# An attention and mixture-of-experts kernel: sums of weight quarters formed earlier and in buffers of their own, a ring of six, and tokens gathered a layer ahead

## The chip, the cores and the metric

The kernel runs as one program on one core of a Trainium2 chip. The metric is device time in microseconds (us) from launch to end. The profiled execution is one run of its own, and its rows give the times at which instructions ran on TensorE (PE, with PEld for the loading of weights), VectorE (DVE), ScalarE (ACT), GpSimd (POOL) and on the issue queue of SyncE (SP).

## The reference

Inputs are float32. Attention on pooled keys and values makes 4608 tokens of 512; each token goes to one of 8 experts (576 tokens each), whose two layers are applied; then a third, common layer with a squared relu and a last product follow.

```python
def _attn_ref(q, k, v):                       # B=8, H=8, S=576, D=64, pool=8
    k_p = k.reshape(B, H, Sp, pool, D).mean(axis=3)
    v_p = v.reshape(B, H, Sp, pool, D).mean(axis=3)
    scores = scale * np.matmul(q, k_p.transpose(0, 1, 3, 2))
    ...
    return np.matmul(attn, v_p)
def _moe_ref(x, w_gate, w1, w2):              # N=4608, D=512, E=8, F=1024
    cap = N // E
    logits = x @ w_gate
    order = np.argsort(-logits.flatten())
    ...                                       # greedy: best pairs first, cap tokens an expert
    for e in range(E):
        mask = assigned == e
        out[mask] = np.maximum(x[mask] @ w1[e], 0.0) @ w2[e]
def _moe2_ref(x, w_in, w_out):                # 512 -> 2048 -> 512
    r = np.maximum(x @ w_in, 0.0)
    return (r * r) @ w_out
```

## The kernel before

**Stages.** `attention` writes the tokens to memory and the gate's logits to `L`; then `mlp(n)` runs for the experts n = 0 to 7, one after the other. Every number that enters a product is split into two float16 parts, and each product takes three passes (`PASSES`). Layer 1 (weights `e1`, tokens `xy`) and layer 2 (weights `e2`, hidden values `hs`) are matrix products through `layer`, line 1250. Layer 3 multiplies by the common `w_in`; its result `g` is multiplied by `w_out` (tile `wo`) in `last_layer`, line 1438, and the rows are scattered to the output.

**Layer 3.** Expert 0 computes it as a plain product with the parts of `w_in` in the tile `wi`. Experts 1 to 7 use a Strassen-Winograd scheme with seven products instead of eight for each of 4 column groups (`ORDER`, `FACTORS`, function `product`, line 1382); their results are put together on ACT (`copy`, `relu`) and DVE (`join` line 1403, `square` line 1408). The scheme needs four sums of quarters of `w_in`. `mix_first` forms them once: 16 pieces, each read from memory (`begin`, line 721), added up on POOL (lines 744 to 747), split by ACT (732) and POOL (733) and stored to `mixed_weights` (737). Layer 3 then reads its weights from there through a ring of `WS` buffers (`fetch_sum`, line 1274). The pieces, the ring and the gathered tokens all lie in the space of `wi`, which expert 0 needs until its layer 3 ends; so `mix_first` waits for `("l3", 0)`, and expert 1 waits for `"mixed"` ahead of its layer 3.

**Background work.** While products run, generators give out other work: `routes` (which tokens go to expert n; small DVE steps with a matmul between them, lines 808 to 1050), `feed` and `fetch(n)` (the expert's weights: loads line 1069, squares on ACT 1079, a column sum on PE 234, splitting on ACT 1092 and DVE 1093, first w1, and then w2 through the same buffer `hs`), and `tokens` and `gather(n)` (gathering by POOL line 1156, splitting 1189 and 1190 into `gfm`, transposing by DMA 1191). The buffer `hs` is also the one that layer 1 writes its result to.

**What sets the order.** All engines work in the order in which the code gives out instructions. The class `Background` keeps an estimate of how far PE, ACT, DVE and POOL have come (`pe`, `a`, `v`, `p`). `tick` advances a task while its engines are no more than `depth` us ahead of PE by this estimate; a task names its engines ("av" for `feed` and `tokens`, "rv" for `routes`, "ap" for `mix_first`). In layer 3 `depth` is `NEAR` = 1.2, most ticks hold back tasks that use ACT (`hold="a"`), and `slot(0.9)` and `slot(3.0)` open all tasks once a group each. `wait_next(n)` stands ahead of each expert's layer 1: it gives out what is still missing of the expert's w1, w2 and tokens.

## Time and profile before

| | us |
|---|---|
| median of 3 runs | 1467.92 (1464.05 to 1469.99) |
| profiled execution, its own time | 1471.88 |
| its span, first to last instruction | 1469.4 |
| PE busy | 1310.9 (89%) |
| DVE busy | 906.6 (62%) |
| ACT busy | 636.3 (43%) |
| POOL busy | 444.9 (30%) |

The attention stage takes about the first 190 us; expert 0 runs from 236 us, expert 1 from 407 us, expert 2 from 594 us, and expert 7 starts at 1319 us. A row of the timeline gives start, length, engine, line, what is written and read, and in square brackets how long the engine had stood still just ahead of it and what ended that.

### The profile page before, as it was taken

Reading aid. Unit: us, or ns where it says so; the run is one execution under the profiler, and the core shown is the slowest. Engines: PE = TensorE matmul, PEld = TensorE weight load, DVE = VectorE, ACT = ScalarE, POOL = GpSimd, SP = SyncE. Lnnn points to the kernel's source line nnn. Section 1 sums busy time; section 2 is a strip of 40 time slices with the busy share of each in tenths; the row PEclk is TensorE's granted clock in tenths of the full one; section 3 lists DMA queues with packets and bytes.
Section 4 is the critical chain, followed back from the end, with each engine's and each line's share of the span. In section 5 each row is a group of like instructions: output and inputs, shape, how many; then the busy total and the mean of one; then the engine's idle time right before and its main releaser. Section 6 shows DMA issues by size and latency. Waiting matters only on the chain.

```text
span 1469.4 us, 25459 instructions
## 1 busy us (share of the span) xinstructions
PE 1310.9 (89%) x9925; PEld 928.7 (63%) x9925; DVE 906.6 (62%) x2203; ACT 636.3 (43%) x1241; POOL 444.9 (30%) x449
## 2 busy tenths in 40 slices
PE   6999927989794798998899789999999999999997
PEld 5989826765373653775367535774677477647753
DVE  6797997888477684678667966473246314622520
ACT  4776756544433452144433442264336414632520
POOL 4552041235556341024302431143015102510430
PEclk8997957999897899999999999999999999999999
DMA  8877457003644634023531451064314602470400
GB/s 339 331 307 271 172 186 234 1 1 112 169 101 118 187 116 119 8 72 130 138 84 58 145 156 60 1 201 136 87 53 153 197 15 83 147 191 4 129 30 21
DMA packets 138872, 186.09 MB, mean 127 GB/s; under 512 B 74624, under 2 KB 88960, under 8 KB 134016
## 3 DMA queue, kind: packets, MB, share of 16 engines
q1 hardware_dynamic: 127744, 156.15, 33.8%
q0 software_dynamic: 5824, 18.88, 3.9%
q10 hardware_dynamic: 5184, 9.44, 1.7%
q8 instruction: 77, 1.26, 0.4%
q14 instruction: 43, 0.35, 0.1%
HBM read 143.67 MB, written 30.41 MB: 118 GB/s over the span
## 4 chain that ended last, share of the span: by engine, by line
PE 56%; DVE 16%; ACT 5%; issue 4%; DMA 3%; POOL 2%; SPq 0%; POOLq 0%; ACTq 0%; DVEq 0%
PE mm L1250 22%; PE mm L1438 20%; PE mm L1382 13%; DMA xy<-gfm 3%; DVE qa L1408 2%; DVE gep L855 1%; DVE gfm L1190 1%; DVE qa L1403 1%; ACT gfm L1189 1%; DVE e L1093 1%; POOL wi L733 1%; DVE hs L1285 1%; DVE rf L851 1%; DVE wi L1408 1%; DVE rfb L859 0%
## 5 line engine op out<-in xcount | busy, mean ns | idle before, releaser
L1438 PE MATMUL mm<-wo,g 128*128 128x512 f16 x1728 | 393.3, 387 | 0.0
L1250 PEld LDWEIGHTS <-e 128*128 128x128 f16 x3024 | 292.4, 98 | 76.0 <-issue 2.5
L1438 PEld LDWEIGHTS <-g 128*128 128x128 f16 x1728 | 169.0, 100 | 217.9 <-issue 24.6
L1382 PEld LDWEIGHTS <-wi 128*128 128x128 f16 x2352 | 229.5, 98 | 89.3 <-issue 29.0
L1250 PE MATMUL mm<-hs,e 128*128 128x288 f16 x1536 | 193.2, 286 | 0.0
L1382 PE MATMUL mm<-wi 128*128 128x288 f16 x1344 | 178.5, 287 | 14.6 <-DVE wi L1403 10.9
L1250 PE MATMUL mm<-xy,e 128*128 128x288 f16 x1488 | 186.4, 286 | 1.1 <-DVE hs L1285 1.1
L1382 PE MATMUL mm<-xy,wi 128*128 128x288 f16 x1008 | 136.3, 289 | 11.5 <-issue 11.1
L1415 POOL TENSOR_TENSOR g<-qa,g 128x576 f16<-128x576 f32 x70 | 99.4, 1426 | 104.8 <-ACT g L1414 100.6
L1285 DVE SCALAR_TENSOR_TENSOR hs<-mm,hs 128x576 f16<-128x576 f32 x64 | 48.1, 754 | 90.7 <-ACT hs L1284 90.7
L1449 POOL DMA_INDIRECT out_dram<-qa,idx x32 | 33.2, 1038 | 228.8 <-ACT qa L1446 228.4
L1284 ACT ACTIVATE hs<-mm 128x576 f16<-128x576 f32 x64 | 41.6, 651 | 130.3 <-PE mm L1250 124.8
L1093 DVE SCALAR_TENSOR_TENSOR e<-hs,e_s,e 128x1024 f16<-128x1024 f32 (+1 forms) x64 | 75.9, 1234 | 27.0 <-ACT e L1092 26.1
L1408 DVE SCALAR_TENSOR_TENSOR qa<-qa 128x576 f32<-128x576 f32 x86 | 76.6, 892 | 13.0 <-ACT qa L1395 8.1
L1399 ACT ACTIVATE qa<-mm,sg_s 128x576 f32<-128x576 f32 x72 | 52.9, 736 | 66.9 <-PE mm L1250 20.2
L1446 ACT ACTIVATE qa<-mm,uo 128x512 f32<-128x512 f32 x32 | 21.9, 685 | 137.1 <-PE mm L1438 122.3
L1079 ACT ACTIVATE e<-hs 128x1024 bf16<-128x1024 f32 x60 | 62.7, 1046 | 38.3 <-DMA hs<-in_w_dram 37.0
L451 ACT ACTIVATE es<-sc,mb 128x72 f32<-128x72 f32 x288 | 64.7, 337 | 31.3 <-DVE mb L449 30.9
L1415 POOL TENSOR_TENSOR g<-wi,g 128x576 f16<-128x576 f32 x42 | 56.8, 1352 | 70.6 <-ACT g L1414 70.6
L1190 DVE SCALAR_TENSOR_TENSOR gfm<-wi,x_s,gfm 128x512 f16<-128x512 f32 (+1 forms) x35 | 26.0, 749 | 81.7 <-ACT gfm L1189 81.5
L1403 DVE SCALAR_TENSOR_TENSOR qa<-mm,sg_s,qa 128x576 f32<-128x576 f32 x56 | 45.5, 813 | 47.2 <-ACT qa L1399 42.3
L1092 ACT ACTIVATE e<-hs,e_s 128x1024 f16<-128x1024 f32 (+1 forms) x64 | 65.8, 1084 | 15.0 <-DVE e_n L223 11.7
(357 smaller groups left out, 1894.2 us busy)
## 6 DMA issues: line engine op xcount, KB each, us to landing
wi<-mixed_weights SPq DMA_DIRECT2D x196, 256.0 KB, 3.1
hs<-in_w_dram SPq DMA_DIRECT2D x60, 512.0 KB, 6.3
tokens_dram<-x ACTq DMA_DIRECT2D x36, 256.0 KB, 4.7
kt<-in_k_dram SPq DMA_DIRECT2D x7, 1152.0 KB, 8.5
vt<-in_v_dram SPq DMA_DIRECT2D x7, 1152.0 KB, 11.3
qt<-in_q_dram SPq DMA_DIRECT2D x7, 1152.0 KB, 5.6
mixed_weights<-wi SPq DMA_DIRECT2D x56, 128.0 KB, 2.0
e<-in_win_dram SPq DMA_DIRECT2D x6, 1024.0 KB, 9.6
```

What stands on the lines that cost most here:

```text
L451: A.activation(es[i][:, x, :], sc[i, x // 4][:, x % 4, :], AF.Exp, scale=1.0 / 64.0, bias=mb[:, x:x + 1])
L1079: A.activation(dst[:, 0, s2, :].bitcast(BF), staged(st, j)[:, s2, :], AF.Square, accum_out=rm[:, c:c + 1])
L1092: A.activation(dst[:, 0], src, AF.Copy, scale=s)
L1093: V.scalar_tensor_tensor(dst[:, 1], src, s, dst[:, 0], op0=OP.mult, op1=OP.subtract)
L1250: T.matmul(p[:, z, 0:HT], lhsT=lh, rhs=mov(b, c)[:, HALVES[z]], start=c == 0 and a + b == 0, stop=c == kk - 1 and a == 1)
L1285: V.scalar_tensor_tensor(halved(h[:, 1, m]), p, 0.0, halved(h[:, 0, m]), op0=OP.max, op1=OP.subtract)
L1382: T.matmul(p[:, z, 0:HT], lhsT=w[:, k, u, z * 128:z * 128 + 128], rhs=yq[:, k, v], start=i in (1, 2, 5) and k == 0 and u + v == 0, stop=k ...
L1399: A.activation(q, p, AF.Copy, scale=sg["r"])
L1403: V.scalar_tensor_tensor(q, p, sg["r"], q, op0=OP.mult, op1=OP.add)
L1408: V.scalar_tensor_tensor(q, q, 0.0, q, op0=OP.max, op1=OP.mult)
L1415: P.tensor_tensor(out=g[:, 1, m:m + 2, gz], in0=q, in1=g[:, 0, m:m + 2, gz], op=OP.subtract)
L1438: T.matmul(o2[c], lhsT=g[:, b, kk, cs], rhs=wo[:, kk // 2, a, kk % 2, :], start=z == 0 and a + b == 0, stop=z == 15 and a == 1)
```

## The change

The buffer `mixb` (three tiles of 128 x 512 float32) is new. `mix_first` puts the pieces there: two buffers for reading, the third for the split sums. It no longer waits for the end of expert 0's layer 3 before it starts on the pieces, only before the first ring loads. Each piece is stored by one DMA whose rows are 256 numbers long instead of two with 128; `product` reads the sums with their indices in the new order. The ring has 6 buffers; the two that fall out and `mixb` hold the gathered tokens from expert 2 on (`xg2`), so `gather(n)` for n > 1 can start ahead of the end of the previous layer 3, and its splitting is spaced by 4 us. `Background` has a second limit, `vdepth`, on DVE alone: 0.9 in layer 3 of experts 1 to 7 and 9.9 elsewhere; `depth` is no longer lowered there.

```diff
-WS = 8
+WS = 6
...
-                   and all(getattr(self, e) <= self.pe + self.depth for e in t[3] if e != "r")):
+                   and all(getattr(self, e) <= self.pe + (min(self.depth, self.vdepth) if e == "v" else self.depth)
+                           for e in t[3] if e != "r")):
...
-    xgs = [wflat.bitcast(F32)[:, o:o + DM] for o in (4096, 4608, 5120, 5632, 6976)]
+    mixb = wt.tile([128, 3, DM], F32)
+    xg1 = [wflat.bitcast(F32)[:, o:o + DM] for o in (4096, 4608, 5120, 5632, 6976)]
+    xg2 = [wflat.bitcast(F32)[:, o:o + DM] for o in (3072, 3584)] + [mixb[:, z] for z in range(3)]
...
-        while ("l3", 0) not in done:
-            yield later()
...
+        parts = mixb[:, 2].bitcast(F16).rearrange("p (s a f) -> p s a f", s=4, a=2)
...
+        for n, (gr, k, z) in enumerate(pieces):
+            flat = mixb[:, n % 2].rearrange("p (q f) -> p q f", q=4)
...
             bg.work(p=2.1)
-            if n:
-                convert(n - 1)
             yield bg.p + 2.0
-        convert(len(pieces) - 1)
+            A.activation(parts[:, :, 0], flat, AF.Copy)
+            P.tensor_tensor(out=parts[:, :, 1], in0=flat, in1=parts[:, :, 0], op=OP.subtract)
+            bg.work(a=0.6, p=1.4)
+            o = k * 512 + z * 256
+            nc.sync.dma_start(out=mix[gr, 3:7, :, o:o + 256].rearrange("s p f -> p s f"),
+                              in_=parts.rearrange("p s a f -> p s (a f)"))
+            yield bg.p
+            if n + 2 < len(pieces):
+                begin(n + 2)
+        while ("l3", 0) not in done:
+            yield later()
...
-        while ("l3", n - 1) not in done:
-            yield later()
+        if n == 1:
+            while ("l3", 0) not in done:
+                yield later()
         for _ in range(NM + 1):
             get()
+        if n > 1:
+            while ("l3", n - 1) not in done:
+                yield later()
+            at = [max(at[c], bg.pe + 4.0 * c) for c in range(NM + 1)]
...
                 if k == 0:
-                    bg.depth = NEAR
                     bg.tick(0.73, hold="a")
...
         b, a, e = mm(), mm(), mm()
+        bg.vdepth = 0.9
...
-            bg.depth = NEAR
             bg.tick(hold="a")
-        bg.depth = DEPTH
+        bg.vdepth = 9.9
```

On POOL, in layer 3 of expert 0, the low parts of `g` (line 1485 before, 1488 after) stood in one row, with the sums behind them (744 to 747, and 733 for the split). Before:

```order
L1485 TENSOR_TENSOR g<-qa,g 128x576 x16
L1156 DMA wi<-tokens_dram,idx_4764 128x512 x4
L1156 DMA wi<-tokens_dram,idl_3141 64x512
L744 TENSOR_TENSOR wi<-wi 128x128
L745 TENSOR_TENSOR wi<-wi 128x128
L746 TENSOR_TENSOR wi<-wi 128x128
L747 TENSOR_TENSOR wi<-wi 128x128
```

After (730 to 733 are the additions, 737 is the split):

```order
L1488 TENSOR_TENSOR g<-qa,g 128x576 x2
L737 TENSOR_TENSOR mixb<-mixb 128x4x128
L1488 TENSOR_TENSOR g<-qa,g 128x576 x2
L730 TENSOR_TENSOR mixb<-mixb 128x128
L731 TENSOR_TENSOR mixb<-mixb 128x128
L732 TENSOR_TENSOR mixb<-mixb 128x128
L733 TENSOR_TENSOR mixb<-mixb 128x128
L1488 TENSOR_TENSOR g<-qa,g 128x576 x2
```

The pieces now lie between the low parts; 8 of the 16 stand ahead of the gathering of expert 1's tokens, and the last one stands in the middle of expert 1's layer 2.

On DVE, in the first column groups of expert 1's layer 3, the splitting of expert 2's w1 (1093) stood between the steps that put the results together (1403 and 1408 before, 1406 and 1411 after). Before:

```order
L1403 SCALAR_TENSOR_TENSOR qa<-mm_2617,sg_s,qa 128x576
L1408 SCALAR_TENSOR_TENSOR qa<-qa 128x576
L1408 SCALAR_TENSOR_TENSOR wi<-wi 128x576
L1408 SCALAR_TENSOR_TENSOR qa<-qa 128x576
L1093 SCALAR_TENSOR_TENSOR e_139<-hs,e_s,e_139 128x1024
L1403 SCALAR_TENSOR_TENSOR wi<-mm_2617,sg_s,wi 128x576
```

After:

```order
L1406 SCALAR_TENSOR_TENSOR qa<-mm_2617,sg_s,qa 128x576
L1411 SCALAR_TENSOR_TENSOR qa<-qa 128x576
L1411 SCALAR_TENSOR_TENSOR wi<-wi 128x576
L1411 SCALAR_TENSOR_TENSOR qa<-qa 128x576
L971 TENSOR_TENSOR roq<-rqi,row 128x576
L1406 SCALAR_TENSOR_TENSOR wi<-mm_2617,sg_s,wi 128x576
```

No splitting of weights stands there any more; a step of the routing does.

On SP, from expert 3's layer 3 to the next expert, the loads of expert 4's w1 (1069 before, 1063 after) stood among the ring loads (1274 before, 1273 after). Before:

```order
L1274 DMA wi<-mixed_weights 128x1024 x7
L1115 TENSOR_LOAD ei_8131
L1115 ISA x2
L1069 ISA
L1069 DMA hs<-in_w_dram 128x1024
...
L1274 DMA wi<-mixed_weights 128x1024 x13
```

After:

```order
L1273 DMA wi<-mixed_weights 128x1024 x28
L1190 DMA_TRANSPOSE xy<-gfm 128x8x128
L1109 TENSOR_LOAD ei_8364
L1109 ISA x2
L1063 ISA
L1063 DMA hs<-in_w_dram 128x1024
...
L1190 DMA_TRANSPOSE xy<-gfm 128x8x128 x3
```

The loads now stand behind the last ring load and the first transpose, so they start when layer 3 is over; this holds at each of the six steps from expert 1 on (at expert 1 the loads stand ahead of all five transposes).

On PE, at the start of expert 3's layer 1, the column sum of w2 (234 before, 236 after) stood some 55 matmuls, of `w_out` and of the routing, ahead of layer 1. Before:

```order
L1438 MATMUL mm_2616<-wo,g 128x512
L234 LDWEIGHTS onesb
L234 MATMUL rp<-rsm_8657,onesb 128x1
L876 LDWEIGHTS gep
L876 MATMUL rp<-oh,gep 128x64
```

After:

```order
L1441 MATMUL mm_2617<-wo,g 128x512
L236 LDWEIGHTS onesb
L236 MATMUL rp<-rsm_8648,onesb 128x1
L1249 LDWEIGHTS e_139
L1249 MATMUL mm_2616<-xy,e_139 128x288
```

It now stands directly ahead of layer 1, as it does for experts 5 and 7; for experts 2, 4 and 6 37 to 48 matmuls still lie between.

## Rows read from the trace of the kernel before

**Rows 1.** Stretches: us, busy of PE, PEld, DVE, ACT, POOL, clock, DMA.
```profile
264.00:350.00 86.00, 76.63 (x651) 59.04 (x649) 74.00 (x186) 36.22 (x56) 30.39 (x22) 0.98 0.02 4
455.00:482.00 27.00, 1.85 (x24) 1.04 (x22) 19.26 (x42) 8.92 (x16) 16.87 (x22) 0.58 0.55 153
```
**Rows 2.** Waits of PE: who waited for whom, us in total, times, longest.
```profile
PE rp L234 <- DVE rsm L230: 11.0, 5, 2.8
PE mm L1382 <- DVE wi L1403: 10.9, 5, 3.5
...
PE mm L1382 <- DVE qa L1403: 3.7, 3, 1.8
```
**Rows 3.** Timeline of PE, end of expert 1's layer 2 to its layer 3.
```profile
453.16 2.37 PE L1250 MATMUL mm<-hs,e 128*128 128x288 f16 x18
...
481.98 1.60 PE L1382 MATMUL mm<-xy,wi 128*128 128x288 f16 x6 [11.09 <-issue]
...
483.66 3.83 PE L1382 MATMUL mm<-xy,wi 128*128 128x288 f16 x18
```
**Rows 4.** Timeline of POOL in the same place, the last splits.
```profile
476.18 2.26 POOL L733 TENSOR_TENSOR wi<-wi 128x512 f16<-128x512 f32 x2 [5.63 <-ACT wi L732]
```
**Rows 5.** Timeline of DVE and of PE in expert 1's layer 3.
```profile
497.95 2.04 DVE L1093 SCALAR_TENSOR_TENSOR e<-hs,e_s,e 128x1024 f16<-128x1024 f32 x1 [1.42 <-ACT e L1092]
...
500.77 2.37 PE L1382 MATMUL mm<-wi 128*128 128x288 f16 x18 [1.40 <-DVE wi L1403]
```
**Rows 6.** Timeline of DVE and of PE in expert 2's layer 3.
```profile
685.16 2.50 DVE L977 TENSOR_TENSOR roq<-rqi,row 128x576 bf16<-128x576 int32 x2
...
688.44 3.04 PE L1382 MATMUL mm<-wi 128*128 128x288 f16 x12 [3.51 <-DVE wi L1403]
```
**Rows 7.** Timeline of PE in the products of `w_out` between experts.
```profile
568.03 0.28 PE L890 MATMUL rp<-rcd,onesh 120*128 120x120 f16 x1 [6.81 <-DVE rcd L885]
...
728.73 0.23 PE L890 MATMUL rp<-rcd,onesh 120*128 120x120 f16 x1 [2.70 <-DVE rcd L885]
...
877.55 0.28 PE L890 MATMUL rp<-rcd,onesh 120*128 120x120 f16 x1 [4.90 <-DVE rcd L885]
877.63 6.51 PE L1438 MATMUL mm<-wo,g 128*128 128x512 f16 x18
...
1026.36 14.59 PE L1438 MATMUL mm<-wo,g 128*128 128x512 f16 x60
```
**Rows 8.** Timeline of SP, DVE and PE between the later experts.
```profile
1138.02 3.98 SPq L1069 DMA_DIRECT2D hs<-in_w_dram  x4
1151.40 10.69 SPq L1191 DMA_TRANSPOSE xy<-gfm  x5
...
1032.38 4.87 DVE L1093 SCALAR_TENSOR_TENSOR e<-hs,e_s,e 128x1024 f16<-128x1024 f32 x4 [5.44 <-ACT e L1092]
...
1161.02 23.47 PE L1438 MATMUL mm<-wo,g 128*128 128x512 f16 x108
...
1319.40 23.68 PE L1250 MATMUL mm<-xy,e 128*128 128x288 f16 x192
```
**Rows 9.** Timeline of SP and of DVE: expert 1's weights, first load to last split.
```profile
347.57 2.13 SPq L1069 DMA_DIRECT2D hs<-in_w_dram  x4
...
402.66 4.87 DVE L1093 SCALAR_TENSOR_TENSOR e<-hs,e_s,e 128x1024 f16<-128x1024 f32 x4
```
**Rows 10.** Single lines: count, ns min/median/max, first and last start.
```profile
L859 DVE SCALAR_TENSOR_TENSOR rfb<-rkm,rfb x42: 145/152/2069, 191.6 to 892.6; 128x1 int32<-128x1 int32 x42
...
L744 POOL TENSOR_TENSOR wi<-wi x16: 452/465/1431, 364.8 to 468.4; 128x128 f32<-128x128 f32 x16
...
L733 POOL TENSOR_TENSOR wi<-wi x16: 1152/1158/1663, 371.7 to 477.3; 128x512 f16<-128x512 f32 x16
```
**Rows 11.** DMA: ring loads (KB, median us to landing); weight loads from 1080 to 1160 us.
```profile
wi<-mixed_weights SPq DMA_DIRECT2D x196, 256.0 KB, 3.1
...
DMA to landing us min/median/max: 4.9/6.6/8.9
```

More of the change, by code (lines that the diff above doesn't have):

```diff
@@ L68, in __init__ @@
         self.depth = DEPTH
+        self.vdepth = 9.9
     def add(self, gen, uses="av"):
@@ L618, in moe_kernel @@
     wflat = wi.rearrange("p c a b f -> p (c a b f)")
-    ring = [wflat[:, z * 1024:z * 1024 + 1024].rearrange("p (k a f) -> p k a f", k=2, a=2) for z in range(WS)]
+    ring = [wflat[:, z * 1024:z * 1024 + 1024] for z in range(WS)]
     yt = wflat[:, 8192:8192 + 16 * HT].rearrange("p (t k a f) -> p t k a f", t=4, k=2, a=2)
@@ L709, in mix_first @@
             yield bg.pe + 1.0
-        while ("l3", 0) not in done:
-            yield later()
         pieces = [(gr, k, z) for gr in range(4) for k in range(2) for z in range(2)]
-        stage = {}
+        parts = mixb[:, 2].bitcast(F16).rearrange("p (s a f) -> p s a f", s=4, a=2)
         def begin(n):
             gr, k, z = pieces[n]
-            o = 512 * (n % 4)
-            stage[n] = wflat.bitcast(F32)[:, o:o + 512].rearrange("p (a b f) -> p a b f", a=2, b=2)
             o = gr * 256 + z * 128
             for a in range(2):
-                nc.sync.dma_start(out=stage[n][:, a], in_=rows4[k, :, a, :, o:o + 128])
+                nc.sync.dma_start(out=mixb[:, n % 2].rearrange("p (a b f) -> p a b f", a=2, b=2)[:, a],
+                                  in_=rows4[k, :, a, :, o:o + 128])
         begin(0)
@@ L725, in mix_first @@
         yield bg.pe + 8.0
-        def convert(n):
-            gr, k, z = pieces[n]
-            o = 4096 + 1024 * (n % 4)
-            parts = wflat[:, o:o + 1024].rearrange("p (a s f) -> p a s f", a=2, s=4)
-            flat = stage.pop(n).rearrange("p a b f -> p (a b) f")
-            A.activation(parts[:, 0], flat, AF.Copy)
-            P.tensor_tensor(out=parts[:, 1], in0=flat, in1=parts[:, 0], op=OP.subtract)
-            bg.work(a=0.6, p=1.4)
-            for a in range(2):
-                o = k * 512 + a * 256 + z * 128
-                nc.sync.dma_start(out=mix[gr, 3:7, :, o:o + 128].rearrange("s p f -> p s f"), in_=parts[:, a])
-        for n in range(len(pieces)):
-            if n + 2 < len(pieces):
-                begin(n + 2)
-            st = stage[n]
-            a11, a21, a12, a22 = (st[:, a, b] for a in range(2) for b in range(2))
+        for n, (gr, k, z) in enumerate(pieces):
+            flat = mixb[:, n % 2].rearrange("p (q f) -> p q f", q=4)
+            a11, a21, a12, a22 = (flat[:, q] for q in range(4))
             P.tensor_tensor(out=a22, in0=a21, in1=a22, op=OP.add)
@@ L1147, in get @@
             if n:
-                t = xgs[c]
+                t = (xg1 if n == 1 else xg2)[c]
             elif c == NM:
-                t = r_p.tile([128, DM], F32, name="xg", bufs=1)
+                t = mixb[:, 2]
             else:
@@ L1273, in fetch_sum @@
         gr, i = ORDER[j]
-        nc.sync.dma_start(out=ring[j % WS].rearrange("p k a f -> p (k a f)"), in_=mix[gr, FACTORS[i][0]])
+        nc.sync.dma_start(out=ring[j % WS], in_=mix[gr, FACTORS[i][0]])
     def mlp(n, arrive=None):
@@ L1377, in product @@
             p = {1: b, 2: a, 3: e, 4: b, 5: e, 6: b, 7: b}[i]
-            w, yq = ring[j % WS], ysum[FACTORS[i][1]]
+            ia, iy = FACTORS[i]
+            w, yq = ring[j % WS], ysum[iy]
+            if ia < 3:
+                w = w.rearrange("p (k a z f) -> p k a z f", k=2, a=2, z=2)
+            else:
+                w = w.rearrange("p (k z a f) -> p k a z f", k=2, a=2, z=2)
             for k in range(2):
@@ L1381, in product @@
                     for u, v in PASSES:
-                        T.matmul(p[:, z, 0:HT], lhsT=w[:, k, u, z * 128:z * 128 + 128], rhs=yq[:, k, v],
+                        T.matmul(p[:, z, 0:HT], lhsT=w[:, k, u, z], rhs=yq[:, k, v],
                                  start=i in (1, 2, 5) and k == 0 and u + v == 0, stop=k == 1 and u == 1,
```

## The prediction

> **What bounds the kernel now.** I read the stretches first, then the waits of PE, then the timeline around each long wait. From expert 0 on, PE is the engine that sets the end: it is busy in nearly every stretch, and the time to be won lies where it stands still. The largest such place is one: from 455 to 482 us PE works 1.85 of 27 us, at a mean granted clock of 0.58 [rows 1]. Layer 2 of expert 1 ends at 453.16 + 2.37 = 455.5 and the first product of its layer 3 starts at 481.98 [rows 3]. What ends last there is POOL's two splits of the last pieces at 476.18 to 478.4 [rows 4], behind which the stores and the first ring loads follow (median 3.1 us to landing, [rows 11]). So 26.4 us pass because the sums of weights are made too late, not because any engine is full.
>
> Smaller standstills repeat. In layer 3 of experts 1 to 3, PE waits eight times, 10.9 + 3.7 = 14.6 us, for `join` on DVE [rows 2]; the rows show what is ahead of it there: a split of w1 of 2.04 us in expert 1 [rows 5], two routing steps of 2.50 us together in expert 2, with a wait of 3.51 [rows 6]. Between the experts PE waits five times, 11.0 us, for the squares of w2 behind the column sum [rows 2], and for routing steps held up on DVE: 6.81, 2.70 and 4.90 us [rows 7]. After some of these the products are slow for a while: 18 take 6.51 us and 60 take 14.59 [rows 7], where 108 take 23.47, 0.217 each, in an undisturbed row [rows 8].
>
> **The change part by part.** All sums go against the profiled execution: 1471.9 us for a span of 1469.4; the median of the three runs, 1467.9, is 4.0 lower, and I carry the same difference over.
>
> *Sums formed earlier.* The code's order puts the last piece 124 of layer 2's matmuls ahead of its end (at 23.68/192 = 0.123 us each, the rate of layer 1, [rows 8], about 15 us), and the first ring loads right behind it. Store and load then need some 6 us of these 15. The whole wait goes: 26.4 us less the 1.85 that PE worked, hence 24.6; and the 24 slow products behind it (1.60 + 3.83 us against 24 x 0.123 = 2.95, [rows 3]) give back 2.5. **Minus 27.1.** What is late next there is nothing that I find: the scale of layer 3 needs the result of layer 2, as before.
>
> *POOL beside expert 0.* A piece costs POOL 4 x 0.465 + 1.158 = 3.0 us [rows 10], and eight pieces, 24 us, now lie in the time from 264 to 350, where POOL has 86 - 30.4 = 55.6 us free [rows 1]. POOL itself is covered. DVE is not: it works 74.0 of these 86 us [rows 1], with routing steps that PE waits for. That DVE instructions can be held far beyond their own time shows in line 859: median 0.152 us, longest 2.069 [rows 10]. Bounds: none of POOL's 24 us reaches DVE and nothing is lost (the pieces also leave the time after 360, where they could hold DVE too), or all of it does, 24. Nearest is the median of line 859, which says that most instructions are not held: I take a quarter. **Plus 6.** The ACT copy waits for POOL's four additions and for the last store out of the one buffer; queued behind it on ACT are the results of layer 3, for which PE has three tiles of room, so I price it at nothing beyond the 6.
>
> The Trainium skill (SBUF — State Buffer, section SBUF: two separate sides) says that VectorE with two inputs in SBUF and a GpSimd instruction that reads SBUF take a shared pair of ports by an exclusive lock, held for the whole instruction, with the loser blocked. This speaks against the change. The row of line 859 agrees with the kind of delay, though not with every instruction being hit; by the rule alone the term would be near its upper bound, which is a rival below.
>
> *The limit on DVE and the weight loads.* In layer 3 the four splits of w1 (4.87/4 = 1.2 us each by [rows 8], one of 2.04 in [rows 5]) no longer stand ahead of `join`, and routing steps get at most 0.9 us of lead; `slot(3.0)` no longer lets DVE run 3 us ahead. Of the 14.6 us I take back 11; bounds 0 (the routing steps that remain, such as those in [rows 6], hold `join` as long as before) and 14.6. **Minus 11.** The routing work that lay in the gap and in layer 3 moves to other places: DVE worked 19.26 us in the gap [rows 1]. Bounds 0 and 19; as the splits of w1 free 4 x 1.2 us of DVE in the same layer 3, and DVE is idle for 38% of the span, it is nearer to none. **Plus 3.**
>
> *Between the experts.* `fetch` wants room on ACT and on DVE, and in layer 3 it no longer finds it; so w1 is loaded only when layer 3 is over. The chain from there: about 3 us to the first transpose, behind which SP issues the four loads (2 us); 8.9 us for the slowest landing [rows 11]; squares, column sum and scale, some 3; splits of w1, 4.9 on DVE [rows 8], with w2's loads issued behind each; 8.9 for the last of them; squares and sum, some 2: 32 to 33 us to w2's column sum. PE has 174 products of `w_out` left ahead of experts 3, 5 and 7, 37.8 us at 0.217, and 222 ahead of 2, 4 and 6, 48.2 us. The sum fits, by 5 us where it is closest. Then the splits of w2 take 5 to 6 us more; they hold `hs`, into which layer 1 writes, but PE has three tiles of 23.68/8 = 2.96 us, 8.9 us, before it needs a result. In exchange the five transposes no longer come in a row: now they take 10.69 us on SP [rows 8], and the squares and routing steps queued behind their splitting on ACT and DVE are late. Gone with that: the 11.0 us of [rows 2], the 4.90 and 2.70 and the slow products behind them (6.51 - 18 x 0.217 = 2.6; 14.59 - 60 x 0.217 = 1.6) of [rows 7], together 22.8. The 6.81 ahead of expert 2 stays, because there the five transposes still follow each other. New waits: 2 us at the column sum directly ahead of experts 3, 5 and 7. That would be minus 16.8; I take **minus 15**, with bounds of minus 22.8 and of plus 49 (second rival).
>
> *The rest costs nothing:* one store of 256 instead of two of 128 numbers a row (off the path once the wait is gone); the ring of six, because a load of 3.1 us has five products of 12 x 0.123 = 1.5 us to land, and no weight loads stand between ring loads any more; the early gathering, which waits in its own buffers.
>
> Sum: -27.1 + 6 - 11 + 3 - 15 = -44.1. 1471.9 - 44.1 = 1427.8 as a profiled run, 1423.8 by the median. I predict 1425.
>
> **The rivals.** *Only the wait goes.* DVE's work is the same, so the small standstills turn up elsewhere: -27.1 + 6 + 3 = -18, 1450. For it: routing steps have to be done by the same experts' starts. Against it: line 859 starts for the last time at 892.6 us [rows 10], so the steps to experts 5, 6 and 7 have no routing and PE waits there all the same, up to 2.8 us each [rows 2].
>
> *The weight chain is too slow (the slower side).* Expert 1's chain took 60.0 us in this trace, from the first load at 347.57 to the last split at 402.66 + 4.87 [rows 9]. If every later one took that, layer 1 could not go on: 37.8 + 8.9 = 46.7 us are there ahead of experts 3, 5 and 7 and 57.1 ahead of 2, 4 and 6, so 3 x 13.3 + 3 x 2.9 = 49 us are lost and none of the 15 is won: -27.1 + 6 - 11 + 3 + 49 = +20, 1488. It decides from 29 us on, 4.9 for each of the six. Against it: in the stretch of [rows 9] transposes, pieces and POOL's gathering all lie in the chain; two landings and two rounds of splits make 33.
>
> *POOL holds DVE in expert 0.* By the lock the term is 24, not 6: 1443. The Trainium skill's SBUF page, named above, is the rule for it.
>
> *The change doesn't do what it says.* The pieces come late again, because POOL, ACT and the one buffer of split sums delay each other by over 9 us beyond the estimates in the code (15 us less store and load). Up to 20 of the 27 come back: 1445.
>
> *All of it works.* Without the 6 and the 3, and with both bounds won: -27 - 15 - 23 = -65, 1403.
>
> **How the numbers follow.** Forecast 0.61 (1408 to 1438), only the wait 0.17, lock 0.07, late sums 0.04, weight chain 0.05, all of it 0.06. The range of 1404 to 1452 leaves out the weight chain, about a third of "only the wait" and half of "all of it", 0.14. A measurement of this kernel can tell about 0.5%, 7 us, from no change: faster than 1460.6 is 0.93, within is 0.03 (between "only the wait" and the weight chain), slower 0.04.
>
> **What would show it.** PE goes from layer 2 to layer 3 of expert 1 without 5 us of standstill, and the waits of PE for `join` are under 5 us in all; the column sums of w2 wait 0 to 3 us each; in the stretch of expert 0's layer 3, PE is at most 10 us longer than before. Wrong it would be if PE waits over 5 us for column sums or for `hs` at each expert, if DVE's rows in expert 0's layer 3 grow to 1 us and more in number, or if the ring loads come late.

## The result and the profile after

| | before | after |
|---|---|---|
| median of 4 runs, us | 1465.99 (1462.85 to 1469.99) | 1420.55 (1418.14 to 1426.09) |
| profiled execution's span, us | 1469.4 | 1416.4 |

The ratio is 0.9694, with a 95% interval of 0.9655 to 0.9733: 45.4 us less. The forecast was 1425, in a range of 1404 to 1452.

The profiled executions lie 53.0 us apart, more than the medians. The first stage (attention), whose code is the same, accounts for most of the difference: expert 0's first product starts at 235.90 us before and at 229.52 after. So I compare from that product to the end of PE's last one, and by stage. Every number of this table is the difference of two starts in PE's timeline (the first product of layer 1, of layer 3 or of `w_out`); only the tail, expert 7's `w_out`, and the last row end with PE's last product.

| us | before | after | difference |
|---|---|---|---|
| expert 0, layers 1 to 3 | 113.9 | 119.0 | +5.1 |
| expert 1, layers 1 to 3 | 121.8 | 93.4 | -28.4 |
| experts 2 to 4, layers 1 to 3 | 280.5 | 284.4 | +3.9 |
| experts 5 to 7, layers 1 to 3 | 258.0 | 258.0 | 0 |
| the seven stages of `w_out` between experts | 395.2 | 368.0 | -27.2 |
| tail | 54.9 | 54.9 | 0 |
| from expert 0's first product to the end | 1224.4 | 1177.7 | -46.7 |

The stop ahead of expert 1's layer 3 [rows 3, 4] is gone. In the timeline of after, POOL's last split, the ring loads on SP and PE around the end of layer 2 (start, length, engine, line, operation; in brackets the idle time ahead):

```profile
440.21 1.16 POOL L737 TENSOR_TENSOR mixb<-mixb 128x512 f16<-128x512 f32 x1
...
441.80 27.18 SPq L1273 DMA_DIRECT2D wi<-mixed_weights  x15
...
452.08 2.37 PE L1249 MATMUL mm<-hs,e 128*128 128x288 f16 x18
454.28 2.49 PE L1386 MATMUL mm<-xy,wi 128*128 128x288 f16 x19
457.51 0.77 PE L1386 MATMUL mm<-xy,wi 128*128 128x288 f16 x5 [0.74 <-DVE xy L1324]
```

The last split starts 14.2 us ahead of the end of layer 2 (452.08 + 2.37 = 454.45), and layer 3 follows without a stop. PE's waits (engine and line, who was waited for: us in total, times, longest), to be set beside [rows 2]:

```profile
PE mm L1386 <- DVE wi L1406: 7.1, 3, 2.5
...
PE mm L1386 <- DVE qa L1406: 4.3, 4, 2.7
...
PE rp L236 <- DVE rsm L232: 2.7, 2, 1.4
```

The waits for `join` are 7.1 + 4.3 = 11.4 us, hardly less than the 14.6 of before. The waits at column sums fall from 11.0 to 2.7; of these, 1.2 and 1.3 us lie ahead of expert 0, so between the experts 9.8 become 1.4. What a step between later experts looks like now, in the same timeline (before, the second column sum had 2.59 to 2.80 us of waiting ahead of it, for experts 5, 6 and 7):

```profile
956.24 22.18 PE L1441 MATMUL mm<-wo,g 128*128 128x512 f16 x102
...
963.52 1.97 SPq L1063 DMA_DIRECT2D hs<-in_w_dram  x4
...
978.25 0.17 PE L236 MATMUL rp<-rsm,onesb 128*128 128x1 bf16 x1
978.28 17.00 PE L1441 MATMUL mm<-wo,g 128*128 128x512 f16 x78
994.54 0.16 DVE L232 TENSOR_REDUCE rsm<-rmx 128x1 bf16<-128x4 f32 x1 [6.50 <-ACT e L1073]
995.11 0.17 PE L236 MATMUL rp<-rsm,onesb 128*128 128x1 bf16 x1
995.14 2.12 PE L1249 MATMUL mm<-xy,e 128*128 128x288 f16 x16
```

From the first load of w1 (963.52) to w2's column sum (995.11) the chain takes 31.6 us and PE never stands still. It is close: DVE is done with the squares of w2 at 994.54 + 0.16 = 994.70, 0.4 us ahead of the column sum.

### The profile page after: what moved, and what is told of

It reads as the page before. It is cut to its first block, busy times and chain, and to the rows that moved or that the text cites. A ratio compares the mean times of both kernels' runs of the same rounds, so it can differ in the third digit from the quotient of the medians.

```text
span 1416.4 us, 25407 instructions
## 1 busy us (share of the span) xinstructions
PE 1294.5 (91%) x9925; PEld 918.6 (65%) x9925; DVE 910.2 (64%) x2203; ACT 639.1 (45%) x1241; POOL 450.5 (32%) x449
## 4 chain that ended last, share of the span: by engine, by line
PE 57%; DVE 19%; issue 4%; ACT 4%; DMA 1%; POOL 1%; SPq 0%; POOLq 0%; ACTq 0%; DVEq 0%
PE mm L1249 21%; PE mm L1441 19%; PE mm L1386 15%; DVE gep L849 2%; DVE qa L1411 2%; DVE e L1087 1%; DMA xy<-gfm 1%; DVE qa L1406 1%; DVE rf L845 1%; DVE hs L1284 1%; DVE rcd L879 1%; DVE wi L1411 1%; DMA hs<-in_w_dram 0%; DVE rpa L889 0%; DVE wo L656 0%
## 5 line engine op out<-in xcount | busy, mean ns | idle before, releaser
L1441 PE MATMUL mm<-wo,g 128*128 128x512 f16 x1728 | 384.6, 381 | 0.0
L1411 DVE SCALAR_TENSOR_TENSOR qa<-qa 128x576 f32<-128x576 f32 x86 | 73.5, 857 | 12.7 <-ACT qa L1398 9.6
L1406 DVE SCALAR_TENSOR_TENSOR qa<-mm,sg_s,qa 128x576 f32<-128x576 f32 x56 | 45.5, 813 | 50.3 <-ACT qa L1402 45.4
L475 PE MATMUL po<-vg,et 72*128 72x73 f32 (+1 forms) x608 | 63.4, 266 | 4.0 <-DVE x L501 3.8
L1417 ACT ACTIVATE g<-qa 128x576 f16<-128x576 f32 x70 | 46.6, 675 | 44.5 <-DVE qa L1411 44.5
## 6 DMA issues: line engine op xcount, KB each, us to landing
vt<-in_v_dram SPq DMA_DIRECT2D x7, 1152.0 KB, 12.2
```

What stands on the lines that cost most here:

```text
L475: T.matmul(p[h // 4][o:o + n, (h % 4) * 73:(h % 4) * 73 + 73], lhsT=et[i][:, h, o:o + n], rhs=vg[b][:, h, :], start=True, stop=True)
L1406: V.scalar_tensor_tensor(q, p, sg["r"], q, op0=OP.mult, op1=OP.add)
L1411: V.scalar_tensor_tensor(q, q, 0.0, q, op0=OP.max, op1=OP.mult)
L1441: T.matmul(o2[c], lhsT=g[:, b, kk, cs], rhs=wo[:, kk // 2, a, kk % 2, :], start=z == 0 and a + b == 0, stop=z == 15 and a == 1)
```

## The experiments

All stage times below are from PE's timelines, as in the table above.

| us | expert 0 | expert 1 | experts 2-4 | experts 5-7 | `w_out`, 0 to 6 | first product to end |
|---|---|---|---|---|---|---|
| before | 113.9 | 121.8 | 280.5 | 258.0 | 395.2 | 1224.4 |
| early sums alone | 119.4 | 92.9 | 282.4 | 258.0 | 393.3 | 1200.8 |
| after | 119.0 | 93.4 | 284.4 | 258.0 | 368.0 | 1177.7 |
| after, late sums | 113.3 | 144.5 | 274.7 | 258.0 | 377.8 | 1223.3 |
| after, old limits | 120.5 | 100.0 | 282.3 | 266.0 | 368.6 | 1192.3 |
| after, old gathering | 119.4 | 95.0 | 283.0 | 258.0 | 378.2 | 1188.5 |
| after, no spacing | 119.2 | 93.5 | 284.6 | 258.0 | 423.4 | 1233.6 |
| after, no spacing, loads first | 120.8 | 97.0 | 282.1 | 258.0 | 398.4 | 1211.1 |
| after, no POOL work | 116.4 | 93.8 | 284.7 | 258.0 | 367.8 | 1175.6 |
| after, narrow stores | 119.2 | 93.4 | 284.5 | 258.0 | 369.0 | 1179.0 |
| after, ring of four | 119.1 | 93.4 | 283.3 | 259.4 | 370.0 | 1180.1 |
| routing held (first addition) | 119.7 | 95.1 | 267.6 | 266.2 | 365.8 | 1169.2 |
| calm (three additions) | 119.8 | 93.5 | 261.7 | 260.1 | 360.3 | 1150.3 |
| calm, expert 1 too | 120.9 | 89.3 | 262.5 | 259.8 | 396.2 | 1183.5 |

**The sums alone.** The kernel before with `mixb` and the new `mix_first`:

```diff
-        while ("l3", 0) not in done:
-            yield later()
...
+        while ("l3", 0) not in done:
+            yield later()
         for j in range(WS):
             fetch_sum(j)
```

> The kernel before with one part of the change: the pieces of the weight sums in their own buffer, started in expert 0 (with the wide stores that go with it). Ring of eight, gathering, order of loads and limits stay as before. If the parts add up, the stop of 26.4 us ahead of expert 1's layer 3 goes, expert 0 from layer 1 to the end of layer 3 is about 5 us longer (113.9 before, 119.1 after the whole change), and the times between the later experts stay as before (column sums of w2 wait 2.6 to 2.8 us ahead of experts 5, 6 and 7): about 1466 - 22 = 1444 us. If the routing work that lay in the stop turns up as new waits of PE, 1450 or more. If the early sums bring the shorter times between experts too, under 1430.

Measured: 1441.4 us (1439.4 to 1449.1), ratio 0.9791 (0.9717 to 0.9865). Expert 1 gives back 28.9 us and expert 0 takes 5.5. Between the experts next to nothing changes (395.2 to 393.3), and the column sums go on waiting. PE's waits of this kernel:

```profile
PE rp L234 <- DVE rsm L230: 16.4, 7, 3.8
...
PE mm L1378 <- DVE wi L1399: 5.3, 4, 1.8
...
PE mm L1378 <- DVE qa L1399: 2.4, 3, 1.6
```

So the parts do separate, and one thing was not in my forecast: the waits for `join` are 5.3 + 2.4 = 7.7 us here, less than before (14.6) and less than after the whole change (11.4). The early sums alone took waits for `join` away, and the limit on DVE, added to them, took no more of these. Layer 3 of experts 1 to 4 is little shorter for it, 178.7 us against 181.5 before and 176.1 after. That the sums shift which routing steps stand there is likely, but not shown by this run. With late sums the limit does count, as the next run shows.

**The sums late again.** The changed kernel with the wait back ahead of the pieces:

```diff
+        while ("l3", 0) not in done:
+            yield later()
         begin(0)
         begin(1)
...
-        while ("l3", 0) not in done:
-            yield later()
         for j in range(WS):
...
+        elif n == 2:
+            while "mixed" not in done:
+                yield later()
```

> The changed kernel with one part undone: the pieces wait for the end of expert 0's layer 3 again (in their own buffers, and the gathering for expert 2 behind them). If the parts add up, a stop of 22 to 27 us returns ahead of expert 1's layer 3 and expert 0 is 5 us shorter again: 1420.5 + 20 = about 1441 us. If the 5 us in expert 0 do not come from the pieces, expert 0 stays at 119 us and the time is about 1446. If the stop is covered by the other parts, under 1430.

Measured: 1464.6 us, ratio 0.9971 (0.9938 to 1.0003). Expert 0 is 5.7 us shorter, as the first reading said. The stop is 75.16 - 25.16 = 50.0 us (start of layer 2 to start of layer 3, less the 25.16 of an unstopped layer 2), twice what I expected. POOL and PE at its end:

```profile
496.16 1.71 POOL L739 TENSOR_TENSOR mixb<-mixb 128x512 f16<-128x512 f32 x1 [0.74 <-DVE rf L845]
...
501.83 3.54 PE L1389 MATMUL mm<-xy,wi 128*128 128x288 f16 x14 [4.49 <-DMA wi<-mixed_weights]
```

The last split starts 20 us later than before (476.18, [rows 4]), although expert 0's layer 3 ended earlier here (344.20 against 349.84), so the new loop is the slower one when nothing covers it. That the single buffer for split sums does it is likely, but not shown. Started in expert 0, the loop has the time. PE's waits for `join` in this kernel:

```profile
PE mm L1389 <- DVE qa L1409: 3.4, 3, 1.4
...
PE mm L1389 <- DVE wi L1409: 0.5, 2, 0.2
```

With the limit and a stop ahead of layer 3 they are 3.9 us, against 14.6 before and 11.4 after, and layer 3 of experts 1 to 4 takes 171.1 us. So the limit took about 11 us of these waits as long as there was a stop, and nothing on top of the early sums: the two parts don't add up. The stop is where routing got ahead: when expert 1's layer 3 starts, 6 of the 16 steps that write `roq` (line 971, 977 before) are done before and here, and 4 after and with the sums alone.

**The old limits.** The changed kernel with `depth` lowered for all engines in layer 3, as before:

```diff
-        bg.vdepth = 0.9
...
+                    bg.depth = NEAR
                     bg.tick(0.73, hold="a")
...
+            bg.depth = NEAR
             bg.tick(hold="a")
-        bg.vdepth = 9.9
+        bg.depth = DEPTH
```

> The changed kernel with the limits of before in layer 3: NEAR for all engines instead of 0.9 us for DVE alone, so that the next expert's w1 is loaded and split in layer 3 again. Early gathering and its spacing stay. If the limit (and the later loads) gives the shorter times between experts, column sums of w2 wait again and 15 to 25 us come back: about 1440 us. If the gathering and its spacing give them, they stay, and only layer 3 changes by a few us: 1417 to 1425.

Measured: 1433.9 us, ratio 0.9727 (0.9643 to 0.9811). `w_out` keeps its 368.6 us, so the limit is not what shortens the times between experts once the gathering is spaced. What is lost lies in layer 3: 309.4 us over experts 1 to 7 against 291.6. PE's waits, and SP and PE in expert 5's layer 3:

```profile
PE mm L1386 <- DMA wi<-mixed_weights: 9.5, 4, 3.4
...
PE mm L1386 <- DVE wi L1407: 8.4, 4, 3.3
```

```profile
1063.68 1.94 SPq L1063 DMA_DIRECT2D hs<-in_w_dram  x4
1065.73 14.08 SPq L1273 DMA_DIRECT2D wi<-mixed_weights  x8
...
1074.67 2.00 PE L1386 MATMUL mm<-wi 128*128 128x288 f16 x12 [3.41 <-DMA wi<-mixed_weights]
```

With a ring of six, four weight loads among the ring loads make PE wait for the ring: 9.5 us in four places. With a ring of eight and the same loads (the sums alone) experts 5 and 6 lose nothing. So the limit on DVE is what pays for the smaller ring, by keeping those loads away from the ring loads; the two kernels differ in the gathering too, and a ring of eight with the new gathering was not run. The waits for `join` are not longer without it: 8.4 us on `wi` and 0.8 on `qa`, 9.2 against 11.4.

**The old gathering.** The changed kernel with `gather` waiting for the end of the previous layer 3, unspaced:

```diff
-        if n == 1:
-            while ("l3", 0) not in done:
-                yield later()
+        while ("l3", n - 1) not in done:
+            yield later()
         for _ in range(NM + 1):
             get()
-        if n > 1:
-            while ("l3", n - 1) not in done:
-                yield later()
-            at = [max(at[c], bg.pe + 4.0 * c) for c in range(NM + 1)]
```

> The changed kernel with tokens gathered as before, only when the previous layer 3 is over, without the spacing of 4 us; the limit on DVE stays. If the limit gives the shorter times between experts, within 5 us of the changed kernel: 1418 to 1425. If the gathering ahead and its spacing give them, 15 to 25 us come back: about 1440. In my prediction the early gathering itself was priced at nothing and the spreading of the transposes was part of the 15 us.

Measured: 1429.0 us, ratio 0.9704 (0.9629 to 0.9779); 10.8 us more than after by stages, between both expectations. `w_out` takes 378.2 us. Put side by side: neither limit nor new gathering 393.3, limit alone 378.2, new gathering alone 368.6, both 368.0. The two do the same work twice.

**No spacing.** The changed kernel, early gathering kept:

```diff
-            at = [max(at[c], bg.pe + 4.0 * c) for c in range(NM + 1)]
```

> The changed kernel without the spacing of 4 us alone: tokens are still gathered ahead of the end of the previous layer 3, but their splits follow each other directly. Tokens gathered with neither (the run with the old gathering) cost 10.7 us from expert 0's start to the end (1188.5 against 1177.7). If the spacing is what matters, most of it is lost here too, 1186 to 1190, and the column sums of w2 wait 1 to 3 us ahead of experts 5 and 7; if having the tokens early matters, 1177 to 1181.

Measured: 1474.3 us in the one run, and 1233.6 from expert 0's first product: 55.9 us more than after and 45.1 more than with the old gathering. Neither number that I had put down comes near. PE's waits, and SP and PE between experts 4 and 5:

```profile
PE rp L236 <- DVE rsm L232: 28.4, 5, 11.7
...
PE rp L870 <- DVE gep L849: 21.9, 9, 12.1
```

```profile
983.00 16.99 SPq L1189 DMA_TRANSPOSE xy<-gfm  x5
1001.12 14.50 SPq L1063 DMA_DIRECT2D hs<-in_w_dram  x6
...
1010.94 0.19 PE L236 MATMUL rp<-rsm,onesb 128*128 128x1 bf16 x1 [11.72 <-DVE rsm L232]
1010.98 2.29 PE L1440 MATMUL mm<-wo,g 128*128 128x512 f16 x5
```

Tokens that are already there are split at once, the five transposes fill SP's queue for 17 us, and the next expert's w1 is loaded behind them. PE then stands for 11.7 us at the first column sum, and the five products behind it take 2.29 us, 0.46 each instead of 0.217, at a granted clock of 0.50 (1.2 GHz). The waits at column sums, 25.7 us more than after, are about half of the 55.9. Of the rest, much is PE waiting at line 870 for routing steps on DVE (21.9 us, 9.5 after), 12.1 us of it in one place. Gathered late, the transposes had stood behind the loads: with the old gathering SP issues the loads between these experts at 951.29 and the transposes at 979.39. Early gathering by itself is a loss; only with the spacing is it worth something.

**No spacing, loads first.** The two tasks change places, so that the loads stand just ahead of the transposes:

```diff
-    bg.add(tokens())
     bg.add(feed())
+    bg.add(tokens())
```

> The kernel without the spacing (1233.6 us from expert 0's start to the end), with the next expert's weight loads given out just ahead of the five token transposes instead of just behind them; nothing else is changed on purpose. In the trace without spacing the first load of w1 is issued at 1001.1 us, behind five transposes that fill 983.0 to 1000.0 on SP's queue, and the column sum of w2 is 11.7 us late. If it is the loads' place behind the transposes that costs, the waits for column sums fall to 0 to 3 us and the time from expert 0's start falls to 1177 to 1192. If the splits and squares standing behind the transposes on ACT and DVE cost, it stays above 1215.

Measured: 1211.1 from expert 0's first product, 22.6 of the 55.9 us back; the number falls between both expectations. PE's waits, and SP, ACT and PE between experts 4 and 5:

```profile
PE rp L870 <- DVE gep L849: 21.6, 7, 11.9
...
PE rp L236 <- DVE rsm L232: 8.6, 3, 5.2
```

```profile
978.90 2.17 SPq L1063 DMA_DIRECT2D hs<-in_w_dram  x4
...
993.70 16.36 SPq L1189 DMA_TRANSPOSE xy<-gfm  x5
...
1007.34 0.72 ACT L1187 ACTIVATE gfm<-mixb,x_s 64x512 f16<-64x512 f32 x1 [6.26 <-DMA mixb<-tokens_dram,idx]
1007.97 1.04 ACT L1073 ACTIVATE e<-hs 128x1024 bf16<-128x1024 f32 x1
...
1012.47 0.19 PE L236 MATMUL rp<-rsm,onesb 128*128 128x1 bf16 x1 [5.21 <-DVE rsm L232]
```

The waits for column sums fall from 28.4 to 8.6 us, so it was the loads' place behind the transposes that made most of them. What is left of them shows in the rows: the loads are issued 15 us before the transposes, yet the column sum waits 5.2 us, because ACT's squares (1073) stand behind the last split of the tokens (1187), which itself had waited 6.26 us for a DMA. But 33.4 us do not come back, and the order on ACT at the column sum is the smaller part of them. The waits for routing steps at line 870 stay as they were, 21.6 against 21.9 us, where after has 9.5: twice what is left at the column sums (8.6 against 2.7). The place on SP is not their cause. At the longest of them the routing steps stand on DVE behind the splits of the tokens, which suggests these as the cause; it was not tried by itself.

**No POOL work on the pieces.**

```diff
+        P.memset(mixb[:, 2], 0.0)
...
-            P.tensor_tensor(out=a22, in0=a21, in1=a22, op=OP.add)
...
-            P.tensor_tensor(out=parts[:, :, 1], in0=flat, in1=parts[:, :, 0], op=OP.subtract)
```

> The changed kernel with POOL's work on the pieces left out: neither the four additions nor the split are done (the low parts are zero, so the weight sums are wrong); loads, ACT's copies, stores and all orders stay. If the longer layer 3 of expert 0 (62.2 us after the change, 57.8 before) comes from POOL holding DVE, it falls back to 56 to 58 us, DVE's 136 instructions there take about 51 us again instead of 57.0, and routing steps lose their stretched durations. If it comes from ACT's copies or from another order of the instructions, it stays at 62.

Measured: 1417.8 us in the one run; layer 3 of expert 0 takes 57.83 us (57.76 before, 62.18 after), layer 2 takes 27.74 (27.74 before, 28.52 after). Layer 1 was 2.4 us longer in this execution, with short waits for its tokens, and the table's 116.4 contains them. The stretches of expert 0's layer 3 in after and in this kernel (start:end and length, then busy us of PE, PEld, DVE, ACT, POOL, clock, DMA):

```profile
286.39:348.57 62.18, 49.92 (x426) 38.30 (x424) 57.01 (x136) 25.96 (x38) 39.93 (x40) 1.00 0.16 45
```

```profile
289.59:347.42 57.83, 51.30 (x426) 39.16 (x424) 49.92 (x132) 25.96 (x38) 20.86 (x14) 0.97 0.14 37
```

ACT does the same 25.96 us of work in both, the loads and stores are there in both. POOL's 19.1 us are gone, and with them 7.1 us of DVE time (four of the 136 DVE instructions fall outside the stretch there). With late sums, where no piece lies in this stretch, the same 136 DVE instructions take 51.01 us. One instruction held, in the timeline of after:

```profile
312.68 1.27 POOL L1488 TENSOR_TENSOR g<-qa,g 128x576 f16<-128x576 f32 x1
312.70 1.28 DVE L845 SCALAR_TENSOR_TENSOR rf<-rkm,rba 128x15 int32<-128x15 int32 x1
314.02 0.72 DVE L849 TENSOR_TENSOR gep<-rm,rf 128x540 bf16<-128x540 f32 x1
...
314.80 0.32 PE L870 MATMUL rp<-oh,gep 128*128 128x64 bf16 x5 [3.05 <-DVE gep L849]
```

Line 845, whose median is 0.175 us, takes 1.28 and ends within 0.03 us of POOL's instruction, with which it started. PE waits for the next one. (POOL's instruction here is a low part of `g`, which stood in this layer before too, but not behind a piece.) The 5.1 us of expert 0 come from POOL's work on the pieces, and by these rows from DVE being held beside it.

The Trainium skill (SBUF — State Buffer, section SBUF: two separate sides) calls this an exclusive lock for the whole instruction, and these rows agree: the one that starts second ends when the first has ended. The prediction's upper bound of 24 us was not reached. In the traces, 33 of the 136 DVE instructions of this stretch take over 0.1 us longer than the shortest of their kind, 14.7 us in all; with late sums it is 14 of them and 8.5 us. So 18.7 us more of POOL work (39.93 against 21.24) lengthened DVE's instructions by 6.2 us: most of POOL's time falls where it holds nothing on DVE.

**Narrow stores.**

```diff
-                nc.sync.dma_start(out=mix[gr, 3:7, :, o:o + 256]...
+            for a in range(2):
+                nc.sync.dma_start(out=mix[gr, 3:7, :, o + a * 128:o + a * 128 + 128]...
```

> The changed kernel with each piece stored in two DMAs with rows of 128 numbers, as before, instead of one with rows of 256. If the stores lie off the path, as my prediction priced them, every stage is within 1 us of the changed kernel. If they hold the one buffer of split sums long enough to delay ACT and POOL, expert 0's layer 3 or expert 1's layer 2 is longer by some us, up to 16 x 1 us in all.

Measured: every stage within 1.1 us of after, 1179.0 in all against 1177.7. The wider stores bring nothing that shows.

**A ring of four.** `WS = 4`.

> The changed kernel with a ring of four instead of six. If a ring load (2.7 us to landing) has only to beat the products ahead of it (four of 1.5 us) and no weight loads stand between ring loads, layer 3 stays within 1 us in each expert and PE never waits for the ring. If six was already at the edge, PE waits for ring loads in each layer 3, 1 us or more.

Measured: 1180.1 us from expert 0's first product; the layers 3 of experts 4 to 7 are 0.3 to 0.6 us longer each. The median of the one run, 1433.2, tells nothing of that: this execution came to expert 0 only at 242.2 us. PE's wait for the ring:

```profile
PE mm L1386 <- DMA wi<-mixed_weights: 1.1, 3, 0.5
```

With no weight loads between, four buffers nearly do; six have room.

**Two stops that are left.** From the trace of after I took two causes: expert 1's tokens, split right behind each other, and routing steps in layer 3. The first, in after (PE's stop of 7.3 us behind DVE, which splits the last of the tokens while SP issues transposes):

```profile
378.09 10.15 SPq L1190 DMA_TRANSPOSE xy<-gfm  x4
...
386.28 0.74 DVE L1189 SCALAR_TENSOR_TENSOR gfm<-wi,x_s,gfm 64x512 f16<-64x512 f32 x1 [1.63 <-ACT gfm L1188]
...
387.83 0.26 PE L884 MATMUL rp<-rcd,onesh 120*128 120x120 f16 x1 [7.29 <-DVE rcd L879]
```

The edit moves the spacing out of `if n > 1` and holds the task of the routing in layer 3:

```diff
-            at = [max(at[c], bg.pe + 4.0 * c) for c in range(NM + 1)]
+        at = [max(at[c], bg.pe + 4.0 * c) for c in range(NM + 1)]
...
-                    bg.tick(0.73, hold="a")
+                    bg.tick(0.73, hold="ar" if n > 1 else "a")
...
-            bg.tick()
+            bg.tick(hold="r" if n > 1 else "")
...
-            bg.tick(hold="a")
+            bg.tick(hold="ar" if n > 1 else "a")
```

> The changed kernel with two additions, meant to take away stops that are left in it: the splitting of expert 1's tokens is spaced by 4 us too, and no routing step is given out in layer 3 of experts 2 to 7. By what the trace of the changed kernel shows, the stop of 7.3 us in the products of w_out after expert 0 is DVE standing behind transposes that follow each other every 2 us; spaced, 5 to 8 us of it go. The waits for `join` in layer 3 of experts 2 and 3 (2.5, 0.5, 2.3 and 2.7 us) are routing steps ahead of it; held back, 6 to 10 us go there, and 0 to 3 come back where the steps go instead. Together 1405 to 1411 us. If the held steps delay the next expert's start, no gain or a loss at experts 3 to 5.

Measured: 1410.8 us (1410.4 to 1413.4), ratio 0.9599 (0.9586 to 0.9613). Layer 3 of experts 2 and 3 falls from 45.06 and 48.26 to 38.51 and 38.50 us: the waits for `join` were routing steps. In after they look like this:

```profile
769.55 2.98 POOL L1418 TENSOR_TENSOR g<-qa,g 128x576 f16<-128x576 f32 x2
769.66 1.75 DVE L849 TENSOR_TENSOR gep<-rm,rf 128x540 bf16<-128x540 f32 x1
771.33 1.22 DVE L853 SCALAR_TENSOR_TENSOR rfb<-rkm,rfb 128x1 int32<-128x1 int32 x1
...
773.61 1.82 PE L1386 MATMUL mm<-wi 128*128 128x288 f16 x9 [2.26 <-DVE wi L1406]
```

Two steps of 0.72 and 0.15 us (the medians) take 1.75 and 1.22 beside POOL, and `join` comes behind them. The first addition did nothing: the stop after expert 0 stays at 7.42 us, because the spacing counts from PE's place and the first tokens are expected 12 us later anyway. And 7.2 us came back in layer 1 of expert 5 (30.74 instead of 23.52), in the manner of expert 3's, whose layer 1 takes 29.53 here and 29.35 in after (24.32 before). In this kernel, ahead of the stop in expert 3:

```profile
696.56 4.88 DVE L1087 SCALAR_TENSOR_TENSOR e<-hs,e_s,e 128x1024 f16<-128x1024 f32 x4 [1.21 <-ACT e L1086]
...
702.24 0.26 PE L884 MATMUL rp<-rcd,onesh 120*128 120x120 f16 x1 [3.33 <-DVE rcd L879]
```

A routing matmul given out at the start of layer 1 waits for DVE, which has the four splits of w2 ahead.

**Calm.** Routing held, expert 1's tokens spaced from the first one on, and DVE's estimate raised after the wait ahead of experts 3, 5 and 7:

```diff
+        if n == 1:
+            at = [max(at[c], at[0] + 3.0 * c) for c in range(NM + 1)]
...
+        if n % 2 and n > 1:
+            bg.v = max(bg.v, bg.pe + 7.0)
```

> The changed kernel with three additions: no routing step in layer 3 of experts 2 to 7 (it took 16 us out of layer 3 of experts 2 and 3 in the previous run); expert 1's tokens split at least 3 us apart counted from the first; and after the wait ahead of experts 3, 5 and 7 the estimate of DVE's lead is set to at least 7 us, so that no routing matmul is given out behind the four splits of w2 (4.9 us on DVE) at the start of layer 1. The stop of 7.4 us after expert 0 should shrink to under 2, and layer 1 of experts 3 and 5 fall from 29.5 and 30.7 to 24 to 25 us: 1169 - 6 - 10 = about 1153 to 1157 from expert 0's start to the end, 1394 to 1400 us in all. If DVE's work merely moves the wait on, 1165 to 1169 and 1406 to 1411.

Measured: 1394.9 us (1392.6 to 1399.8), ratio to before 0.9520 (0.9498 to 0.9542), 25.7 us below the median of the change under study. The stop after expert 0 (7.29 us in after) becomes one of 2.83, layer 1 of experts 3 and 5 takes 23.97 and 24.12 us; from expert 0's first product it is 1150.3, a little better than forecast.

**Calm, expert 1 too.** `hold="ar" if n > 0`.

> As the previous kernel, but routing steps are held back in layer 3 of expert 1 as well. Its layer 3 has waits of 0.8 and 2.4 us for `join`: if it falls from 45 to 38.5 us as in the others, 5 us less in all; but the tokens for experts 2 to 6 are then known only when layer 3 is over, their gathering can't run ahead, and if that decides, 2 to 10 us are lost between the experts.

Measured: 1426.8 us, ratio 0.9744 (0.9711 to 0.9778). Layer 3 of expert 1 falls by 4.3 us, to 39.17, and `w_out` rises by 35.9. Five stops of 6.2 to 8.0 us for routing steps stand between the experts. So holding does not pay here. By what was expected it is because the tokens of the next experts are then known too late; that was not tried by itself.

## Why the prediction was right, step by step

The time was right (1425 forecast, 1420.6 measured), but two of its terms were mis-sized, by about the same amount in opposite directions (+10.6 and -12.2 us). That the sum came out so near is luck.

- **Sums formed earlier, -27.1:** right. Expert 1 gave 28.4 us after the whole change and 28.9 with this part alone. The 15 us of lead were 14.2.
- **POOL beside expert 0, +6:** right in size (5.1) and in cause. The quarter was a choice between 0 and 24; taking POOL's work away took away just these 5.1 us in layers 2 and 3. That the choice came out so near is luck too; the 6.2 us by which DVE's instructions grew show what the quarter stood for. In late sums this layer 3 takes 56.46 us at a granted clock of 1.00, against 57.76 before at 0.97, so the cost at the same clock is up to 1.3 us higher.
- **The limit on DVE, -11, and the moved routing, +3:** wrong. Experts 1 to 4 beyond the first term gave -1.3 + 3.9 = +2.6 instead of -8. The failed step is "in layer 3 the four splits of w1 no longer stand ahead of `join`". They don't, but what stood ahead in most of the waits were routing steps, some of them lengthened beside POOL, and the limit lets them in. The lower bound, 0, was named for this reason, and I should have taken it: of the two rows that I had, one [rows 6] was a routing step. The sum also took the two terms as separate, and they aren't: with the stop left in, 10.7 of the 14.6 us go (late sums); with the stop closed only 3.2 do, and the routing is then 2 steps of `roq` further behind when layer 3 starts. And 5.0 us of the moved routing turn up in layer 1 of expert 3 (24.32 before, 29.35 after), where a routing matmul waits behind the splits of w2; that alone is more than the 3. The sign that I had set, under 5 us of waits for `join`, did not come: there are 11.4.
- **Between the experts, -15:** mis-sized; it gave -27.2, beyond the better bound of -22.8. The chain was forecast at 32 to 33 us from the end of layer 3 to w2's column sum. From 956.24 to 994.70 it was 38.5, because the first load came 7.3 us after that end; it fit with 0.4 us to spare ahead of expert 5, not with 5. The better bound was passed because the 6.81 us ahead of expert 2 did not stay: that stage lost 5.8 us. It does so with the old gathering too (59.39 us against 59.63 after and 64.38 with the sums alone), and with the old limits as well (58.84), so either part alone takes it. And the new waits of 2 us came only ahead of expert 3 (1.39), not ahead of 5 and 7.
- **The rest at nothing:** right for the stores and the ring, and for the ring I gave the reason that the old limits then showed. Wrong for "the early gathering, which waits in its own buffers": without the spacing it costs 45 us against gathering late. It came out as nothing only because I had put the spacing elsewhere in the sum.
- **The rivals:** "only the wait goes" (1450) is excluded by the measured time and by the 27.2 us between the experts, though its mechanism holds in layer 3, where the small standstills did turn up elsewhere. "The weight chain is too slow" (1488) did not happen, but its mechanism exists and is one line away: 1474.3 without the spacing, in good part by w1 loaded behind five transposes. The lock at its full price, 24 us, is excluded by the 5.1, and late pieces by the 14.2 us of lead.

## What to carry to other kernels

Work that is ready early is not free on an in-order engine: without a due time it runs at once, and stands ahead of what the critical chain needs next (45 us here). Price each early step by what is queued behind it on every engine and on the DMA-issuing queue. And where PE waits for an engine that is not full, look at which small step stood ahead and what ran beside it, before shortening the large ones.

## What the runs showed of the hardware

**The first stage varies by 14 us.** Among fourteen profiled executions, all with the same attention stage, expert 0's first product started between 227.8 and 242.3 us. The first 40 us of after and of the ring of four (columns as above; the clock is the third number from the end, as a share of 2.4 GHz):

```profile
0.00:40.00 40.00, 27.27 (x243) 25.29 (x244) 29.02 (x87) 23.49 (x86) 21.39 (x40) 1.00 0.96 376
```

```profile
0.00:40.00 40.00, 27.75 (x151) 25.43 (x152) 24.23 (x69) 18.94 (x67) 19.04 (x37) 0.79 0.87 338
```

The later one had PE at a mean of 0.79 there, hence at 1.2 GHz for part of the time, and did 151 matmuls instead of 243. The clock of these 40 us is not the whole reason: the sums alone had 1.00 there too and came to expert 0 only at 236.60, the old limits had 0.79 and came at 233.65. Why, stays open. Expert 0's layer 1 still varies, from 28.35 to 30.80 us; from its layer 2 on, most stages that a change does not touch repeat to 0.2 us, and they are the better measure here.

**A transpose holds the issuing queue longer than a load of its size.** Lines of SP in after (count, ns min/median/max), a transpose and a ring load:

```profile
L1190 SPq DMA_TRANSPOSE xy<-gfm x35: 1194/1271/4904, 375.3 to 1248.0; - x35
```

```profile
L1273 SPq DMA_DIRECT2D wi<-mixed_weights x196: 319/320/5514, 441.8 to 1346.7; - x196
```

1.27 us against 0.32, for 256 KB in both (128 KB in the last of five transposes). The Trainium skill (Advanced Engine Details and Errata, section X-Bar Transpose (TRN2)) has transposes as fast as regular DMAs. To landing the medians in this trace are 4.3 us for a transpose and 2.7 for a ring load (which reads memory, where the transpose reads the buffer `gfm`), so it does not agree here; of the time on the issuing queue that section says nothing.
